# Row maxima of an attention kernel: split into high and low part on VectorE ahead of their turn, and one fp32r product with an identity in place of an fp32 transposition

## The chip, the core and the metric

The kernel runs on one core of a Trainium2 chip. TensorE multiplies matrices (128 rows by 128 columns of stationary weights, a moving operand of up to 512 columns) and writes to PSUM. VectorE (DVE), ScalarE (ACT) and GpSimd (POOL) do the elementwise work, and SyncE (SP) issues most of the DMAs. Each engine takes its instructions in program order, and semaphores order the engines against each other. The metric is the time of one execution on the device, in microseconds. Before the change it was 838.71 us, the median of three runs (838.14 to 839.35).

## What is computed

With `x` of 2048 x 640, everything in fp32:

```python
xn  = layernorm(x)
# A: 32 heads of 20, a causal window of 256 keys
q, k, v = heads(xn @ wqkv)
p   = softmax(where(0 <= i - j < 256, q @ k.T * 20**-0.5, -1e9))
s   = (p @ v).merge() @ wo
# B: squared ReLU
g   = silu(relu(xn @ w1 + b1)**2 @ w2 + b2)
out = x + s * g
```

## The kernel before

Products that need close to fp32 accuracy are made in fp32r, with each operand split into a rounded high part and a rest (`hi`, `lo`), and three of the four cross products are summed. `P` = 128, `BT` = 512, `HP` = 64.

The attention runs over 16 pairs of heads (`NP`) and 16 tiles of 128 queries (`NT`), 256 steps in all, plus 11 steps in which the last ones run out. A step `s` does four things in this order on TensorE:

- `scores` (L644): for both heads of the pair, the scores of query tile `q` against up to 384 keys, queries in rows. They serve only to find the row maximum.
- `scores_t` (L684), 9 steps later (`LAG`) for the same tile: the scores again, keys in rows. The stationary and moving operands have two rows more than the 60 of the three-part split (62): the two parts of minus the maximum, so that the product comes out as score minus maximum.
- at every fourth step, `max_rows` (L659): the maxima of the four query tiles just finished are turned from a column per tile into rows.
- then "filler": the products of the other linear layers (`halves`, L634), as many as a planner's clock allows, and on some steps a burst of `values` (L725).

The two heads of a pair, and two jobs of the filler, lie in different halves of TensorE's rows: rows 0 to 63 and rows 64 to 127. The two halves work at the same time on different products. Below they are called **the first half** and **the second half** of the array. `both(one, two, cost)` issues a product for each, and charges `cost` to the planner's clock of each half. The order of all instructions is laid down by Python code at build time (`manual_schedule`): `fill(due[s] + ...)` issues filler until the planner's clock has reached the step's due time. `COST` is the planner's assumption of what a product takes, by its moving columns; it is not measured while the kernel runs.

The path of the maxima before the change:

- `maxima` (L652, DVE): adds the mask to the scores, takes the maximum along the row, and reads the accumulator into one column of `mts`, a 128 x 64 tile of which 8 columns are used (4 query tiles, 2 heads). Two such tiles alternate. Each reduction is two DVE instructions, `CUSTOM_DVE_ANT_0` and `DVE_READ_ACCUMULATOR2_ANT`. The reduction also frees the PSUM bank that the next step's `scores` writes into, so that `scores` of step `s` waits for `maxima` of step `s-1`.
- `max_rows` (L659, PE): two fp32 transpositions of 64 x 64, one per half of the rows, into a corner of the PSUM tile `stps` that `scores_t` of the same step uses.
- ACT L665 takes the 8 rows out of PSUM with the sign turned, ACT L666 rounds them to fp32r (high part), POOL L667 subtracts to get the low part, and two DMAs (L669) put both into rows 60 and 61 of each head's half of `qs`, where `scores_t` finds them three steps later.

The PSUM tile `stps` has one buffer, so `scores_t` of the next step waits until ACT has read it (L690, the exponential, and L665).

Of the kernel before, what the change touches and what calls it, by code (L numbers as in the profile page):

```python
# [9 lines left out]
F32 = mybir.dt.float32  # L10
F32R = mybir.dt.float32r
BF16 = mybir.dt.bfloat16
AF = mybir.ActivationFunctionType
ALU = mybir.AluOpType

P = 128
# [9 lines left out]
BT = S // NB  # L26
VW = DH + 1
NPART = 3
KR = NPART * DH
HP = P // 2  # L30
HALF = D // 2
# [7 lines left out]
EARLY_FILL = 0.4  # L39
WARM = 22  # L40
WARM2 = 10
COST = {P: 0.067, 2 * P: 0.12, HALF: 0.147, 3 * P: 0.172, BT: 0.23}
SCALE = DH ** -0.5
PV = 0.2133
TURN = 0.18
# [12 lines left out]
def f32(ap):  # L58
    return ap.bitcast(F32)
# [3 lines left out]
def attn_mlp_kernel(ctx: ExitStack, tc, x, wqkv, wo, w1, b1, w2, b2, out):  # L63
    nc = tc.nc
    PSUM = bass.MemoryType.PSUM
    const = ctx.enter_context(tc.tile_pool(name="const", bufs=1))
# [27 lines left out]
    ident = const.tile([P, P], F32, name="ident")  # L94
    nc.gpsimd.memset(ident, 1.0)
    nc.gpsimd.affine_select(ident, ident, pattern=[[1, P]], compare_op=ALU.is_equal, fill=0.0, base=0, channel_multiplier=-1)
    mask = const.tile([P, 3 * P], F32, name="mask")
# [1 line left out]

    nc.gpsimd.affine_select(mask[:, 0:P], mask[:, 0:P], pattern=[[1, P]], compare_op=ALU.is_gt, fill=NEG, base=0, channel_multiplier=-1)  # L100
    nc.gpsimd.affine_select(mask[:, 2 * P:], mask[:, 2 * P:], pattern=[[-1, P]], compare_op=ALU.is_ge, fill=NEG, base=0, channel_multiplier=1)
    mts = [const.tile([P, HP], F32, name=f"mt{j}") for j in range(2)]
    for t_ in mts:
        nc.gpsimd.memset(t_, 0.0)
    ones = const.tile([2, P], F32, name="ones")
    nc.gpsimd.memset(ones, 1.0)
    eps = const.tile([P, 1], F32, name="eps")
# [12 lines left out]
    qs = [at.tile([P, S], F32R, tag="qs0", name="qs0")]  # L120
# [457 lines left out]
    at2 = ctx.enter_context(tc.tile_pool(name="at2", bufs=2))  # L578
# [16 lines left out]
    def put(j, emit, cost):  # L595
        clock[2] = clock[j]
        clock[j] += cost
        emit()
# [11 lines left out]
    def ahead(emit, cost):  # L610
        while clock[1] <= clock[0] + LEAD:
            if not open_for(backlog):
                clock[1] = max(clock[1], clock[0])
                break
            behind(backlog)
        put(0, emit, cost)
# [7 lines left out]
    def both(first, second, cost):  # L624
        ahead(first, cost)
        put(1, second, cost)
# [9 lines left out]
    def scores(p, q):  # L636
# [5 lines left out]
        def one(hh):  # L642
            o = slice(hh * HP, hh * HP + KR)
            nc.tensor.matmul(ss[hh][:, :nk], qs[i][o, q * P:(q + 1) * P], ks[i][o, k0 * P:k0 * P + nk], start=True, stop=True)  # L644
        both(lambda: one(0), lambda: one(1), COST[nk])
        return ss, nk

    def maxima(p, q, ss, nk):
        for hh in range(2):
            junk = at2.tile([P, 3 * P], BF16, tag="junk", bufs=1, name="junk")  # L650
            m = 4 * hh + q % 4
            nc.vector.tensor_tensor_reduce(out=junk[:, :nk], in0=ss[hh][:, :nk], in1=mask[:, 3 * P - nk:], scale=1.0, scalar=-3.0e38, op0=ALU.add, op1=ALU.max, accum_out=mts[q // 4 % 2][:, m:m + 1])  # L652

    def max_rows(p, g, tps):
        i = p % 2

        def one(j):
            r = slice(j * HP, (j + 1) * HP)
            nc.tensor.transpose(tps[:HP, j, 3 * P:3 * P + HP], mts[g % 2][r, :], ident[r, r])  # L659
        both(lambda: one(0), lambda: one(1), COST[P])  # L660

        def rest():
            row = at2.tile([8, P], F32, tag="row", bufs=1, name="row")
            mrow = at2.tile([8, 2, P], F32R, tag="mrow", bufs=1, name="mrow")
            nc.scalar.activation(row.rearrange("m (j n) -> m j n", j=2), tps[:8, :, 3 * P:3 * P + HP], AF.Copy, scale=-1.0)  # L665
            nc.scalar.activation(mrow[:, 0, :], row, AF.Copy)  # L666
            nc.gpsimd.tensor_sub(mrow[:, 1, :], row, f32(mrow[:, 0, :]))  # L667
            for a in range(2):
                nc.sync.dma_start(f32(qs[i])[KR + a:KR + a + HP + 1:HP, g * BT:(g + 1) * BT].rearrange("h (q n) -> h q n", q=4), f32(mrow)[:, a, :])  # L669
        return rest  # L670

    pts = {}
# [1 line left out]
    def pair_tile():  # L674
        return ptp.tile([P, 2, BT], F32, tag="st", name="stps")

    def scores_t(p, kb):
# [4 lines left out]
        def one(hh):  # L682
            o = slice(hh * HP, hh * HP + KR + 2)
            nc.tensor.matmul(tps[:, hh, :n], ks[i][o, kb * P:(kb + 1) * P], qs[i][o, kb * P:kb * P + n], start=True, stop=True)  # L684
        both(lambda: one(0), lambda: one(1), COST[n])
        return tps, n
# [11 lines left out]
    def bursts(p):  # L698
        return (range(0, 8), range(8, NT)) if p < NP - 1 else [range(4 * g, 4 * g + 4) for g in range(NB)]

    def burst_at(p, kb):
        return next((ts for ts in bursts(p) if ts[-1] == kb), None)
# [10 lines left out]
    def burst_cost(ts):  # L713
        return TURN + PV * max(sum(len(part) for e, _, part in lanes_of(ts) if e == e_) for e_ in range(2))
# [104 lines left out]
    def halves(job, ps, a, b_, first, last, o=0, n=None):  # L819
        n = n or ps.n  # L820
        cost, out = COST[n], ps.tile[:, o:o + n]

# [564 lines left out]
    def stretch(s):  # L1387
        ts = burst_at(*divmod(s - LAG - PLAG, NT)) if s >= LAG + PLAG else None
        return max(0.0, burst_cost(ts) - 1.8) if ts else 0.0

    total = (8 * (KC - 1) * 15 * COST[BT] + 2 * NB * (15 * (WIDE * COST[BT] + 2 * (NFH - WIDE) * COST[MT]) + 8 * 18 * COST[HALF]) + NP * 2 * NT * COST[3 * P] + sum(burst_cost(r) for p in range(NP) for r in bursts(p)))
    pace = (total - sum(stretch(s) for s in range(steps))) / (steps - 1)
# [16 lines left out]
    with tc.manual_schedule(engines={E_.PE, E_.Activation, E_.DVE, E_.Pool, E_.SP}):  # L1409
# [4 lines left out]
        def at_step(n):  # L1414
            return divmod(n, NT) if 0 <= n < NP * NT else None

        for s in range(steps):
# [7 lines left out]
            a, b, e = (at_step(s - lag) for lag in (0, LAG, LAG + PLAG))  # L1425
            if a:
                p, q = a
# [12 lines left out]
            rows = None  # L1440
# [4 lines left out]
            if s % 4 == 0 and 0 < s <= NP * NT:  # L1445
                rows = max_rows((s - 1) // NT, (s - 1) % NT // 4, stp[0] if b else pair_tile())
            if a:
                maxima(*a, *sc)
# [9 lines left out]
            r = e and burst_at(*e)  # L1458
# [41 lines left out]
```

## Time and profile before

| | |
|---|---|
| median of three runs | 838.71 us |
| the profiled execution | 838.47 us, of which the span from the first to the last instruction is 836.7 us |
| granted TensorE clock, mean | 0.999 |
| TensorE matmul busy, share of the span | 827.1 us, 99% |
| VectorE busy | 479.9 us, 57% |
| ScalarE busy | 438.5 us, 52% |
| GpSimd busy | 379.4 us, 45% |
| DMA traffic | 166.44 MB, 199 GB/s |

A matmul's record begins when it is issued to the array and ends by a model, so its duration (0.3 to 0.4 us for the common shapes) is longer than the time after which the next one starts on the same rows. What a product costs is read from the distance between starts on one half. "PEld" is TensorE's weight load. In a row of the timeline, the columns are start, duration (both us), engine, line, operation, the tile written and those read, the shape, and the number of merged instructions.

### The profile page before, as it was taken

To read this page: it belongs to the slowest core of one execution; us is meant where nothing else is said; L and a number is where in the kernel's file an instruction comes from. 1 tells how busy PE (TensorE), PEld (TensorE's weight loads), DVE (VectorE), ACT (ScalarE), POOL (GpSimd) and SP (SyncE) were. 2 spreads that over 40 slices of the span, in tenths; PEclk is the share of its full clock that TensorE was granted. 3 is DMA by queue.
4 is the path that set the end of the run, shared out by engine and by line. 5 is a ranking of instruction groups with operands and counts; after the bars stand their busy time and mean duration, and the time that the engine had idled before them with its cause. 6 is when DMAs were issued, how large, how long until landed. Compare 5 with 4: busy or idle time off the path is not lost.

```text
span 836.7 us, 25540 instructions
## 1 busy us (share of the span) xinstructions
PE 827.1 (99%) x10152; PEld 778.4 (93%) x10152; DVE 479.9 (57%) x1398; ACT 438.5 (52%) x824; POOL 379.4 (45%) x704
## 2 busy tenths in 40 slices
PE   8999999999999999999999999999999999999997
PEld 8999999988888999999999999899999999999997
DVE  7755457656577645455455476754455454446764
ACT  6253325545566754763754765844654744764321
POOL 5167902434334643553543553643543643552543
PEclk9999999999999999999999999999999999999999
DMA  6999578879889456355356254486375375356962
GB/s 236 307 389 341 178 203 277 272 234 288 278 287 307 124 161 174 85 183 144 87 194 183 72 164 143 129 249 175 88 227 172 86 221 171 94 160 207 383 203 80
DMA packets 88944, 166.44 MB, mean 199 GB/s; under 512 B 10360, under 2 KB 36600, under 8 KB 87800
## 3 DMA queue, kind: packets, MB, share of 16 engines
q1 hardware_dynamic: 88664, 164.63, 62.6%
q8 instruction: 80, 1.31, 0.7%
q14 instruction: 40, 0.33, 0.1%
q10 hardware_dynamic: 160, 0.16, 0.1%
HBM read 93.66 MB, written 70.52 MB: 196 GB/s over the span
## 4 chain that ended last, share of the span: by engine, by line
PE 96%; DVE 2%; issue 1%; DMA 0%; ACT 0%; DVEq 0%
PE yps L634 21%; PE hps L634 19%; PE qkps L634 14%; PE ops L725 10%; PE wops L794 8%; PE stps L684 5%; PE sps L644 5%; PE vps L235 4%; PE qkps L210 3%; PE vps L356 3%; PE tps L177 1%; DVE junk L652 1%; DVE w L985 1%; PE vps L411 0%; PE vps L401 0%
## 5 line engine op out<-in xcount | busy, mean ns | idle before, releaser
L652 DVE CUSTOM_DVE_ANT_0 junk<-sps,mask 128x384 bf16<-128x384 f32 (+2 forms) x512 | 272.1, 531 | 255.4 <-PE sps L644 92.4
L690 ACT ACTIVATE p<-stps 128x768 f32<-128x768 f32 (+2 forms) x256 | 197.5, 772 | 249.4 <-PE stps L684 204.7
L691 POOL TENSOR_SCALAR_AFFINE_SELECT p<-p 128x256 f32<-128x256 f32 x256 | 110.4, 431 | 317.5 <-ACT p L690 312.8
L634 PE MATMUL yps<-w,hh 64*128 64x320 f32 x1536 | 224.9, 309 | 1.8 <-ACT relu L1144 0.9
L634 PE MATMUL hps<-xb,w 64*128 64x256 f32 (+1 forms) x2100 | 210.7, 304 | 0.0
L634 PEld LDWEIGHTS hps<-xb,w 64*128 64x128 f32 x2100 | 194.5, 186 | 3.1 <-issue 2.5
L634 PEld LDWEIGHTS yps<-w,hh 64*128 64x128 f32 x1536 | 185.7, 185 | 5.0 <-DVE ysb L1179 1.7
L634 PE MATMUL yps<-w,hl 64*128 64x320 f32 x768 | 175.2, 309 | 0.0
L644 PE MATMUL sps<-ks,qs 60*128 60x384 f32 (+2 forms) x512 | 130.9, 335 | 0.8 <-DVE mt L652 0.6
L684 PE MATMUL stps<-qs,ks 62*128 62x384 f32 (+2 forms) x512 | 127.6, 334 | 0.1
L634 PEld LDWEIGHTS yps<-w,hl 64*128 64x128 f32 x768 | 117.4, 185 | 1.1 <-issue 1.0
L634 PE MATMUL qkps<-xT,wgkh 64*128 64x512 f32 x320 | 100.3, 393 | 0.0
L634 PE MATMUL qkps<-xT,wgqh 64*128 64x512 f32 x320 | 98.5, 392 | 0.0
L693 POOL TENSOR_SCALAR_AFFINE_SELECT p<-p 128x256 f32<-128x256 f32 x224 | 95.9, 428 | 0.0
L725 PE MATMUL ops<-p,vp 128*21 128x128 f32 (+1 forms) x2128 | 86.6, 311 | 0.0
L644 PEld LDWEIGHTS sps<-ks,qs 60*128 60x128 f32 x512 | 81.1, 185 | 5.2 <-DVE mt L652 2.9
L725 PEld LDWEIGHTS ops<-p,vp 128*21 128x21 f32 x2128 | 63.5, 101 | 21.1 <-issue 6.2
L684 PEld LDWEIGHTS stps<-qs,ks 62*128 62x128 f32 x512 | 80.9, 187 | 1.0 <-issue 0.3
L1149 POOL TENSOR_TENSOR hl<-sq,hh 128x512 fp32r<-128x512 f32 x48 | 62.1, 1294 | 17.8 <-ACT sq L1148 17.6
L794 PE MATMUL wops<-wo,oT 128*128 128x320 f32 x384 | 61.9, 310 | 0.0
L634 PE MATMUL qkps<-xT,wgkl 64*128 64x512 f32 x160 | 61.6, 393 | 0.0
L634 PE MATMUL qkps<-xT,wgql 64*128 64x512 f32 x160 | 61.3, 392 | 0.0
(163 smaller groups left out, 1288.8 us busy)
## 6 DMA issues: line engine op xcount, KB each, us to landing
ks<-k_d SPq DMA_DIRECT2D x64, 240.0 KB
qs<-q_d SPq DMA_DIRECT2D x64, 240.0 KB
xb<-xs SPq DMA_DIRECT2D x60, 256.0 KB
k_d<-shm SPq DMA_DIRECT2D x20, 512.0 KB
q_d<-shm SPq DMA_DIRECT2D x20, 512.0 KB
xs<-xT SPq DMA_DIRECT2D x8, 1280.0 KB
y<-ysb SPq DMA_DIRECT2D x28, 320.0 KB
o<-osb SPq DMA_DIRECT2D x64, 128.0 KB
```

What stands on the lines that cost most here:

```text
L210: nc.tensor.matmul(ps, wt[:, c, :], xT[part][b][:, c * BT + t0:c * BT + t0 + n], start=m == 1, stop=m == 3 * KC)
L235: nc.tensor.matmul(ps, xT[xp][b][:, c * BT + t * P: c * BT + (t + 1) * P], wv[wp][:, c, nh * HALF:(nh + 1) * HALF], start=first and m == 0 ...
L634: return nc.tensor.matmul(out, a[r], b_[r], skip_group_check=True, **kw)
L644: nc.tensor.matmul(ss[hh][:, :nk], qs[i][o, q * P:(q + 1) * P], ks[i][o, k0 * P:k0 * P + nk], start=True, stop=True)
L652: nc.vector.tensor_tensor_reduce(out=junk[:, :nk], in0=ss[hh][:, :nk], in1=mask[:, 3 * P - nk:], scale=1.0, scalar=-3.0e38, op0=ALU.add, o ...
L684: nc.tensor.matmul(tps[:, hh, :n], ks[i][o, kb * P:(kb + 1) * P], qs[i][o, kb * P:kb * P + n], start=True, stop=True)
L690: nc.scalar.activation(p32[:, :, :n], tps[:, :, :n], AF.Exp, scale=SCALE)
L691: nc.gpsimd.affine_select(p32[:, :, 0:P], p32[:, :, 0:P], pattern=[[0, 2], [1, P]], compare_op=ALU.is_ge, fill=0.0, base=0, channel_multip ...
L693: nc.gpsimd.affine_select(p32[:, :, 2 * P:], p32[:, :, 2 * P:], pattern=[[0, 2], [-1, P]], compare_op=ALU.is_gt, fill=0.0, base=0, channel ...
L725: nc.tensor.matmul(ot[r0:r0 + VW, c0:c0 + len(part), :], vps[p][:, kb // 4, kb % 4, hh, :], pts[p, kb][:, hh, :].rearrange("p (t n) -> p t ...
L794: nc.tensor.matmul(ps, a, b_, start=j == 0, stop=j == n - 1)
L1149: nc.gpsimd.tensor_sub(hh[1][:, :BT], sq, f32(hh[0]))
```

## The change

- The maxima of one group (4 query tiles, 2 heads) go to a tile `tops` of 8 columns. At every fourth step, right after the last reduction, VectorE copies `tops` to columns 0 to 7 of `parts`, rounded to fp32r, and writes the rest into columns 8 to 15. `parts` is 128 x 128 with zeros elsewhere, set once from a part of the mask that is zero; there is one of it.
- `max_rows` is one fp32r product per half, with `parts` (64 rows x 128 columns) as the stationary operand and a 64 x 64 identity `eye` in fp32r as the moving one. It writes 128 PSUM rows instead of 64; the first 16 are used.
- One ACT instruction takes all 16 rows out. The second ACT instruction and the POOL subtraction are gone. The two DMAs stay.
- The planner charges 0.04 for the product, where it charged 0.067 for the transposition.

```diff
-COST = {P: 0.067, 2 * P: 0.12, HALF: 0.147, 3 * P: 0.172, BT: 0.23}
+COST = {HP: 0.04, P: 0.067, 2 * P: 0.12, HALF: 0.147, 3 * P: 0.172, BT: 0.23}
...
-    mts = [const.tile([P, HP], F32, name=f"mt{j}") for j in range(2)]
-    for t_ in mts:
-        nc.gpsimd.memset(t_, 0.0)
+    tops = const.tile([P, 8], F32, name="tops")
+    parts = const.tile([P, P], F32R, name="parts")
+    nc.scalar.activation(parts, mask[:, P:2 * P], AF.Copy)
+    eye = const.tile([P, HP], F32R, name="eye")
+    for h in (slice(0, HP), slice(HP, P)):
+        nc.scalar.activation(eye[h], ident[h, h], AF.Copy)
...
-            nc.vector.tensor_tensor_reduce(..., accum_out=mts[q // 4 % 2][:, m:m + 1])
+            nc.vector.tensor_tensor_reduce(..., accum_out=tops[:, m:m + 1])
+        if q % 4 == 3:
+            nc.vector.tensor_copy(parts[:, 0:8], tops)
+            nc.vector.tensor_sub(parts[:, 8:16], tops, f32(parts[:, 0:8]))
...
-            nc.tensor.transpose(tps[:HP, j, 3 * P:3 * P + HP], mts[g % 2][r, :], ident[r, r])
-        both(lambda: one(0), lambda: one(1), COST[P])
+            nc.tensor.matmul(tps[:, j, 3 * P:3 * P + HP], parts[r, :], eye[r, :], start=True, stop=True, skip_group_check=True)
+        both(lambda: one(0), lambda: one(1), COST[HP])
...
-            nc.scalar.activation(row.rearrange("m (j n) -> m j n", j=2), tps[:8, :, 3 * P:3 * P + HP], AF.Copy, scale=-1.0)
-            nc.scalar.activation(mrow[:, 0, :], row, AF.Copy)
-            nc.gpsimd.tensor_sub(mrow[:, 1, :], row, f32(mrow[:, 0, :]))
+            nc.scalar.activation(rows.rearrange("m (j n) -> m j n", j=2), tps[:16, :, 3 * P:3 * P + HP], AF.Copy, scale=-1.0)
```

How this moves the instructions is shown for one group, the one whose transposition starts at 430.82 us in the trace. On TensorE, before: the last filler products ahead of the step, the two score products, the two transposed ones, the two transpositions (`x2`), and filler again.

```order
L634 MATMUL yps<-w_0_1_4001,hh 128x320
L644 MATMUL sps<-ks_117,qs_116 128x384 [waits DVE_49] x2
L684 MATMUL stps<-qs_1478,ks_1479 128x384 [waits Activation_49]
L684 MATMUL stps<-qs_1478,ks_1479 128x384
L659 MATMUL stps<-ident,mt_100 64x64 x2
L634 MATMUL yps<-w_0_0_3964,hh 128x320
L634 MATMUL yps<-w_0_0_3964,hl 128x320
```

The same place on TensorE after the change:

```order
L637 MATMUL yps<-w_0_2_4181,hh 128x320
L647 MATMUL sps<-ks_119,qs_118 128x384 [waits DVE_49] x2
L687 MATMUL stps<-qs_1480,ks_1481 128x384 [waits Activation_49]
L687 MATMUL stps<-qs_1480,ks_1481 128x384
L665 MATMUL stps<-eye,parts 128x64 [waits DVE_49]
L665 MATMUL stps<-eye,parts 128x64
L637 MATMUL yps<-w_0_1_3991,hh 128x320
L637 MATMUL yps<-w_0_0_3950,hl 128x320
```

The product stands where the transpositions stood, and it has a wait for VectorE of its own; the transpositions had none. The filler around it is a little further on in its list than before.

On VectorE, before: the last two reductions of the group and the first two of the next, with their accumulator reads, at the same place.

```order
L652 ISA junk,mt_100<-sps,mask 128x384 [waits DVE_49,PE_49]
L652 ISA mt_100 128x1
L652 ISA junk,mt_100<-sps,mask 128x384 [waits DVE_49,PE_49]
L652 ISA mt_100 128x1
L652 ISA junk,mt_101<-sps,mask 128x384 [waits DVE_49,PE_49]
L652 ISA mt_101 128x1
L652 ISA junk,mt_101<-sps,mask 128x384 [waits DVE_49,PE_49]
L652 ISA mt_101 128x1
L1179 TENSOR_TENSOR ysb<-yps,b2t 128x320 [waits PE_49]
```

The same place on VectorE after the change:

```order
L655 ISA junk,tops<-sps,mask 128x384 [waits DVE_49,PE_49]
L655 ISA tops 128x1
L655 ISA junk,tops<-sps,mask 128x384 [waits DVE_49,PE_49]
L655 ISA tops 128x1
L657 CAST parts<-tops 128x8 [waits DVE_49]
L658 TENSOR_TENSOR parts<-tops,parts 128x8 [waits DVE_49]
L1182 TENSOR_TENSOR ysb<-yps,b2t 128x320 [waits PE_49]
L655 ISA junk,tops<-sps,mask 128x384 [waits DVE_49,PE_49]
L655 ISA tops 128x1
```

Two short instructions stand between the last reduction of a group and whatever VectorE does next, and each waits for the one before it on its own engine (`DVE_49`).

On ScalarE, before: the exponential of this step, the two instructions of the maxima, and the exponential of the next step.

```order
L690 ACTIVATE p_7546<-stps 128x768 [waits PE_49]
L665 ACTIVATE row<-stps 8x128 [waits Pool_49]
L666 ACTIVATE mrow<-row 8x128 [waits DMAHW7_49,DMAHW0_49,Activation_49]
L690 ACTIVATE p_7600<-stps 128x768 [waits PE_49]
L690 ACTIVATE p_7647<-stps 128x768 [waits PE_49]
```

The same place on ScalarE after the change:

```order
L693 ACTIVATE p_7533<-stps 128x768 [waits PE_49]
L670 ACTIVATE rows<-stps 16x128 [waits DMAHW7_49,DMAHW0_49]
L693 ACTIVATE p_7582<-stps 128x768 [waits PE_49]
L693 ACTIVATE p_7626<-stps 128x768 [waits PE_49]
L693 ACTIVATE p_7672<-stps 128x2x256 [waits PE_49]
```

One of the two is left, and it no longer waits for GpSimd.

More of the change, by code (lines that the diff above doesn't have):

```diff
@@ L651, in maxima @@
             m = 4 * hh + q % 4
-            nc.vector.tensor_tensor_reduce(out=junk[:, :nk], in0=ss[hh][:, :nk], in1=mask[:, 3 * P - nk:], scale=1.0, scalar=-3.0e38, op0=ALU.add, op1=ALU.max, accum_out=mts[q // 4 % 2][:, m:m + 1])
+            nc.vector.tensor_tensor_reduce(out=junk[:, :nk], in0=ss[hh][:, :nk], in1=mask[:, 3 * P - nk:], scale=1.0, scalar=-3.0e38, op0=ALU.add, op1=ALU.max, accum_out=tops[:, m:m + 1])
+        if q % 4 == 3:
+            nc.vector.tensor_copy(parts[:, 0:8], tops)
+            nc.vector.tensor_sub(parts[:, 8:16], tops, f32(parts[:, 0:8]))
     def max_rows(p, g, tps):
@@ L658, in one @@
             r = slice(j * HP, (j + 1) * HP)
-            nc.tensor.transpose(tps[:HP, j, 3 * P:3 * P + HP], mts[g % 2][r, :], ident[r, r])
-        both(lambda: one(0), lambda: one(1), COST[P])
+            nc.tensor.matmul(tps[:, j, 3 * P:3 * P + HP], parts[r, :], eye[r, :], start=True, stop=True, skip_group_check=True)
+        both(lambda: one(0), lambda: one(1), COST[HP])
         def rest():
-            row = at2.tile([8, P], F32, tag="row", bufs=1, name="row")
-            mrow = at2.tile([8, 2, P], F32R, tag="mrow", bufs=1, name="mrow")
-            nc.scalar.activation(row.rearrange("m (j n) -> m j n", j=2), tps[:8, :, 3 * P:3 * P + HP], AF.Copy, scale=-1.0)
-            nc.scalar.activation(mrow[:, 0, :], row, AF.Copy)
-            nc.gpsimd.tensor_sub(mrow[:, 1, :], row, f32(mrow[:, 0, :]))
+            rows = at2.tile([16, P], F32R, tag="rows", bufs=1, name="rows")
+            nc.scalar.activation(rows.rearrange("m (j n) -> m j n", j=2), tps[:16, :, 3 * P:3 * P + HP], AF.Copy, scale=-1.0)
             for a in range(2):
-                nc.sync.dma_start(f32(qs[i])[KR + a:KR + a + HP + 1:HP, g * BT:(g + 1) * BT].rearrange("h (q n) -> h q n", q=4), f32(mrow)[:, a, :])
+                nc.sync.dma_start(f32(qs[i])[KR + a:KR + a + HP + 1:HP, g * BT:(g + 1) * BT].rearrange("h (q n) -> h q n", q=4), f32(rows)[8 * a:8 * a + 8])
         return rest
```

## The prediction

> **What bounds the kernel now.** First the page: busy shares, then the chain that ended last.
>
> ```profile
> PE 827.1 (99%) x10152; PEld 778.4 (93%) x10152; DVE 479.9 (57%) x1398; ACT 438.5 (52%) x824; POOL 379.4 (45%) x704
> ...
> PE 96%; DVE 2%; issue 1%; DMA 0%; ACT 0%; DVEq 0%
> ```
>
> TensorE is busy throughout and holds 96% of the chain. So what the change takes off ScalarE, GpSimd and the DMA path of the maxima is worth nothing unless TensorE waits for it. What counts is the time that the two products of a group occupy on TensorE, and any time TensorE now has to wait. Next the view of waits, for what TensorE and its weight load wait for.
>
> ```profile
> PEld sps L644 <- DVE mt L652: 2.9, 9, 0.5
> ...
> PEld yps L634 <- ACT relu L1144: 1.4, 2, 0.8
> ```
>
> The waits shown are small (total, count, longest, in us), and the larger one is for VectorE's maxima. But the view counts only time in which no modelled record runs, and records last 0.3 us and more, so waits below that hide in it. They have to be read from starts. Here is one group, first VectorE and then TensorE.
>
> ```profile
> 429.69 0.08 DVE L652 DVE_READ_ACCUMULATOR2_ANT mt<- 128x1 f32 x1
> 429.92 0.56 DVE L652 CUSTOM_DVE_ANT_0 junk<-sps,mask 128x384 bf16<-128x384 f32 x1
> 430.40 0.08 DVE L652 DVE_READ_ACCUMULATOR2_ANT mt<- 128x1 f32 x1
> 430.88 0.56 DVE L652 CUSTOM_DVE_ANT_0 junk<-sps,mask 128x384 bf16<-128x384 f32 x1 [0.40 <-PE yps L634]
> ```
>
> ```profile
> 430.54 0.43 PE L684 MATMUL stps<-qs,ks 62*128 62x384 f32 x1
> 430.65 0.34 PE L644 MATMUL sps<-ks,qs 60*128 60x384 f32 x1
> 430.82 0.22 PE L659 MATMUL stps<-ident,mt 64*64 64x64 f32 x1
> 430.83 0.33 PE L684 MATMUL stps<-qs,ks 62*128 62x384 f32 x1
> 430.85 0.39 PE L634 MATMUL yps<-w,hh 64*128 64x320 f32 x1
> 431.00 0.22 PE L659 MATMUL stps<-ident,mt 64*64 64x64 f32 x1
> 431.03 0.39 PE L634 MATMUL yps<-w,hl 64*128 64x320 f32 x1
> 431.08 0.31 PE L634 MATMUL yps<-w,hh 64*128 64x320 f32 x1
> 431.23 0.30 PE L634 MATMUL yps<-w,hl 64*128 64x320 f32 x1
> ```
>
> The last reduction of the group ends at 429.92 + 0.56 = 430.48, and the transposition in the first half of the array starts only 0.34 us later. It needs nothing more from VectorE: `scores` of that step has already waited for the same reduction. The interval is the time of the products ahead of it.
>
> **The price of the product itself.** After the transposition (430.82) the next product of that half is issued 0.03 us later, but is 0.08 longer than others of its shape (0.39 against 0.31), and the second next starts at 431.08. Two plain products follow each other by 431.23 - 431.08 = 0.15. So the transposition occupies its half for 431.08 - 430.82 - 0.15 = 0.11. An fp32r product of 64 columns isn't in the trace; the nearest has 128.
>
> ```profile
> 188.26 0.22 PE L644 MATMUL sps<-ks,qs 60*128 60x128 f32 x1
> ...
> 188.32 0.39 PE L684 MATMUL stps<-qs,ks 62*128 62x384 f32 x1
> ...
> 188.55 0.22 PE L659 MATMUL stps<-ident,mt 64*64 64x64 f32 x1
> ```
>
> The pattern is the same: the next product is issued 0.06 later, is too long by about 0.05, and the one after it starts 0.23 later, where a 384-column product is normally followed after 0.18 (430.65 to 430.83). A 128-column product thus occupies 0.06 + 0.05 = 0.11 as well. Equal cost at 64 columns of fp32 and 128 of fp32r says that the columns don't set it; I read it as the next product's weight load, which begins when this one starts. The bounds: at the lowest, the 0.08 belongs to the transposition alone and the new product costs 0.03, which saves 64 groups x 0.08 = 5.1 us; at the highest it costs the 0.11 of the 128-column row. I take 0.11, **a gain of 0**.
>
> The stationary operand grows from 64 to 128 columns. Its load is hidden behind a 384-column product ahead of it, but in 15 groups (step 16p + 24, where `scores_t` is at its last tile) that product has 128 columns.
>
> ```profile
> 246.02 0.22 PE L684 MATMUL stps<-qs,ks 62*128 62x128 f32 x1
> ...
> 246.08 0.22 PE L659 MATMUL stps<-ident,mt 64*64 64x64 f32 x1
> 246.11 0.47 PE L634 MATMUL qkps<-xT,wgqh 64*128 64x512 f32 x1
> ```
>
> Today the transposition starts 0.06 after it, so its narrow load fits. With 128 columns the excess of the row above (0.05 to 0.06) comes in: 15 x 0.057 = **0.9 us lost**; at least 0, at most 15 x 0.11 = 1.7.
>
> [...]
>
> **The wait that is added.** The product needs `parts`, which VectorE finishes with a copy and a subtraction after the group's last reduction. Prices of short VectorE instructions come from one operation at two sizes, and the pause before a dependent one from the start of the kernel:
>
> ```profile
> L114 DVE TENSOR_TENSOR xT<-tps,xT 128x512 fp32r<-128x512 f32 x15 | 9.2, 680 | 1.1 <-ACT xT L113 1.1
> ...
> L471 DVE TENSOR_TENSOR xT<-tps,xT 128x128 fp32r<-128x128 f32 x4 | 1.1, 280 | 0.0
> ```
>
> ```profile
> 6.01 0.11 DVE L455 RECIPROCAL rstd<-rstd 128x1 f32<-128x1 f32 x1
> 6.15 0.61 DVE L162 TENSOR_SCALAR xn<-xt,mv,rstd 128x640 f32<-128x640 f32 x1
> ```
>
> (680 - 280) / 384 = 1.04 ns per column, so 8 columns take 280 - 120 x 1.04 = 155 ns; the reciprocal of one column, 110, is the lower neighbour. A dependent instruction starts 0.03 after an ordinary one (6.15 - 6.12), but 0.15 after an accumulator read (429.77 to 429.92). From the end of the reduction: 0.15 + 0.155 + 0.035 + 0.155 = 0.50. From there to TensorE I take what `scores` needs in the next rows, 0.06 (449.78 to 449.84), and then the load of 128 columns, 0.11. The product can start to work about **0.66 us after the last reduction**. Short end: 0.03 + 0.08 (a read) + 0.03 + 0.155 + 0.06 + 0.11 = 0.47. Long end: 0.85, with 0.2 for each instruction and 0.15 for both pauses.
>
> Where does the transposition stand today? Three groups:
>
> ```profile
> 449.22 0.56 DVE L652 CUSTOM_DVE_ANT_0 junk<-sps,mask 128x384 bf16<-128x384 f32 x1
> ...
> 449.84 0.44 PE L644 MATMUL sps<-ks,qs 60*128 60x384 f32 x1
> ...
> 450.12 0.22 PE L659 MATMUL stps<-ident,mt 64*64 64x64 f32 x1
> ```
>
> ```profile
> 625.23 0.56 DVE L652 CUSTOM_DVE_ANT_0 junk<-sps,mask 128x384 bf16<-128x384 f32 x1
> ...
> 626.18 0.22 PE L659 MATMUL stps<-ident,mt 64*64 64x64 f32 x1
> ```
>
> ```profile
> 496.71 0.56 DVE L652 CUSTOM_DVE_ANT_0 junk<-sps,mask 128x384 bf16<-128x384 f32 x1
> ...
> 498.57 0.22 PE L659 MATMUL stps<-ident,mt 64*64 64x64 f32 x2
> ```
>
> The distance is 450.12 - 449.78 = 0.34 in the first, 0.39 in the second, 1.30 in the third. Over all 64 groups the first half's distance runs from 0.34 to 1.30: 26 groups lie below 0.46, none between 0.46 and 0.58, and 33 below 0.66. In those, TensorE reaches the product before `parts` is there, and it takes its instructions in order: behind the waiting product stand its twin in the second half and all filler, so both halves run dry. Taking 0.66 less the distance wherever positive gives 8.1 us in the first half. The second half's transposition comes later (450.29, not 450.12), so with 0.68 it loses in 23 groups only, 3.0 us. Which counts? The halves' starts stay in program order, and the earlier half loses mostly a lead that it would have given up at the next point where both meet; so I go near the later one and take **3.5 us**. With the short end, 0.47, the sums are 2.8 and 0.03; with the long end, 15.8 and 8.5.
>
> **The rest.** VectorE gets 64 x 0.35 = 22 us more, at 57% busy. Its next reductions and PSUM evacuations come up to 0.35 later at those 64 places; TensorE's own wait covers this in the groups above, and elsewhere VectorE idles there (0.40 us before the reduction at 430.88). If that cover were gone, a late free bank would cost up to 0.3 each time. ScalarE loses one instruction per group and GpSimd one:
>
> ```profile
> L666 ACT ACTIVATE mrow<-row x64: 308/310/312, 123.4 to 734.5; 8x128 fp32r<-8x128 f32 x64
> L667 POOL TENSOR_TENSOR mrow<-row,mrow x64: 442/451/458, 123.9 to 735.1; 8x128 fp32r<-8x128 f32 x64
> ```
>
> That is 20 and 29 us of work off engines that TensorE seldom waits for, and rows that arrive 0.7 us sooner, three steps ahead of their use: 0, at most the 2 us or so that the view of waits shows for ScalarE. The two DMAs stay and no longer hold SP for GpSimd: 0. The planner's 0.067 - 0.04, 64 times, lets 1.7 us of filler go out earlier; the work is the same, the places shift: 0, plus or minus 1.
>
> **Sum.** Against the profiled execution (836.7 span, 838.47 in all): 0 + 0.9 + 3.5 = +4.4, 842.9. The median of the runs is 0.24 higher, so **843.1 us**.
>
> **Rivals.**
> (A) Not slower: the wait is there but hidden, since the chain is near its short end and lost time is made up within the half. Against it speaks the 0.15 after an accumulator read; for it, that only the first half is exposed at 0.47. It gives 838.7 + 0.03 + 0.9 = 839.6, no change.
> (B) The other side: the 0.08 is the transposition's own, and an fp32r product costs 0.03. Its place is the first product after each transposition, its price 64 x 0.08 = 5.1 us, and it decides as soon as more is saved than waits cost (4.4). With the waits as forecast it gives 838.0, with the short end 834.5. The 128-column row speaks against it. [...]
> (C) The chain is near its long end: 8.5 + 0.9 gives 848.1. A longer start of the copy would do it.
>
> **How the numbers follow.** Forecast 0.55, A 0.27, B 0.10, C 0.08. A measurement of this kernel can tell 0.2%, 1.7 us. The forecast and C are slower (0.63); A is within (0.26, with a little of B); B's lower part and a rest are faster (0.11). The range takes in the forecast, A, the upper part of B and C up to its centre: 837.0 to 848.0; about 0.15 lies outside.
>
> **What would show it.** In the profile of the changed kernel: the product's start after the last reduction never under about 0.5 us (now 0.34), with many groups bunched there; products following it still about 0.08 too long; copy and subtraction near 0.15 each with 0.15 ahead of the copy; TensorE's span in the attention longer by some us, ACT and POOL busy 20 and 29 us less. It is wrong if the bunch lies at 0.35, if the next product after it starts without delay, or if VectorE's reductions move so late that whole steps shift.

## The result, and the profile after

The changed kernel takes **857.05 us**, the median of five runs (856.88 to 858.63), against 838.71 us before. The ratio, taken over all runs of both, is 1.0225, with a 95% interval of 1.0214 to 1.0236: 18 to 20 us slower, where +4.4 was forecast. The profiled execution took 857.06 us, with a span of 855.3 us at a mean granted clock of 1.0 (0.999 before), so the clock has no part in it. Of the experiments below, two of the eleven executions of the product alone without the selects ran at a granted clock of 0.56 and 0.57 and took 1341.28 and 1313.63 us, and they are left out of its comparison. First the page of the changed kernel: busy times, and the chain that ended last, by engine and by line.

```profile
PE 841.1 (98%) x10152; PEld 785.1 (92%) x10152; DVE 514.2 (60%) x1526; ACT 423.6 (50%) x764; POOL 346.4 (40%) x638
...
PE 90%; DVE 8%; issue 1%; DMA 0%; ACT 0%; DVEq 0%
PE yps L637 18%; PE hps L637 18%; PE qkps L637 13%; PE ops L728 10%; PE wops L797 8%; PE sps L647 4%; PE vps L238 4%; DVE junk L655 4%; PE stps L687 4%; PE qkps L213 3%; PE vps L359 3%; DVE parts L657 1%; PE stps L665 1%; DVE parts L658 1%; PE tps L180 1%
```

The share that says most is VectorE's in the chain: 8%, from 2%. The copy (L657) and the subtraction (L658) stand in it by name, and so do the reductions ahead of them (L655). VectorE is busy 514.2 - 479.9 = 34 us longer, for 128 short instructions that were forecast at 64 x 0.35 = 22 us. ScalarE is busy 438.5 - 423.6 = 15 us less and GpSimd 33 us less, and the time is longer all the same.

Next the waits of TensorE and its weight load in the changed kernel (total us, count, longest).

```profile
PEld stps L665 <- DVE parts L658: 12.9, 31, 1.1
PEld yps L637 <- DVE ysb L1182: 3.9, 8, 0.8
...
PE stps L665 <- DVE parts L658: 1.7, 6, 0.9
```

The wait for `parts` is there, 31 times and up to 1.1 us. A second line has also grown: filler that waits for a PSUM evacuation (`ysb`), 3.9 us where it was 1.7. What the two added instructions take is in the view of the tile `parts` (duration in ns: shortest, median, longest).

```profile
L665 PEld LDWEIGHTS stps<-eye,parts x128: 182/183/188, 122.5 to 753.1; 64*128 64x128 f32 x128
L665 PE MATMUL stps<-eye,parts x128: 189/293/295, 122.6 to 753.1; 64*128 64x64 f32 x128
L657 DVE CAST parts<-tops x64: 170/367/851, 121.9 to 752.3; 128x8 fp32r<-128x8 f32 x64
L658 DVE TENSOR_TENSOR parts<-tops,parts x64: 166/316/1179, 122.1 to 752.7; 128x8 fp32r<-128x8 f32 x64
```

The shortest are near the 155 ns of the prediction; the medians are twice that. An operation of fixed shape whose time runs from 170 to 851 is being held by something. Here is one group of the changed kernel in the timeline, the one whose step stood at 430.82 us before.

```profile
439.08 0.56 DVE L655 CUSTOM_DVE_ANT_0 junk<-sps,mask 128x384 bf16<-128x384 f32 x1
...
439.56 0.08 DVE L655 DVE_READ_ACCUMULATOR2_ANT tops<- 128x1 f32 x1
439.63 0.41 POOL L694 TENSOR_SCALAR_AFFINE_SELECT p<-p 128x256 f32<-128x256 f32 x1 [3.16 <-ACT p L693]
439.68 0.39 DVE L657 CAST parts<-tops 128x8 fp32r<-128x8 f32 x1
...
439.99 0.41 POOL L696 TENSOR_SCALAR_AFFINE_SELECT p<-p 128x256 f32<-128x256 f32 x1
440.00 0.33 PE L687 MATMUL stps<-qs,ks 62*128 62x384 f32 x1
440.10 0.32 DVE L658 TENSOR_TENSOR parts<-tops,parts 128x8 fp32r<-128x8 f32 x1
...
440.34 0.48 DVE L1182 TENSOR_TENSOR ysb<-yps,b2t 128x320 f32<-128x320 f32 x1
440.47 0.18 PEld L665 LDWEIGHTS stps<-eye,parts 64*128 64x128 f32 x2 [0.46 <-DVE parts L658]
440.47 0.30 PE L665 MATMUL stps<-eye,parts 64*128 64x64 f32 x2
440.58 0.19 PEld L637 LDWEIGHTS yps<-w,hh 64*128 64x128 f32 x1
```

Read it downwards. The reduction ends at 439.64 and the copy starts at 439.68, almost at once. But GpSimd has been in its first select (L694, it masks the exponentials) since 439.63. That ends at 440.04, and the copy ends at 440.07. The subtraction starts 0.03 later, under the second select (L696), which ends at 440.40; the subtraction ends at 440.42. Each ends 0.02 to 0.03 after a select does. So it is with all that are long: 50 of the 64 copies and 48 of the 64 subtractions took over 200 ns, all 98 started while a GpSimd instruction was running, and all ended 16 to 29 ns after it (96 times a select, twice a longer subtraction of GpSimd's, `hl`, L1152). TensorE's weight load, idle for 0.46, starts at 440.47: 0.83 after the last reduction, which is also the median over the 64 groups. With 0.11 for the load, counted to the start of the next one (440.47 to 440.58; the load's own record lasts 0.18), the product works from 0.94 on, by estimate; 0.66 was forecast.

The lengths of the steps, worked out from the first start of `scores` in each and summed by the step's place in a group of four (without the very first step), show where the time is. The step of the product is number 0; the bursts of `values` make step 2 the longest.

| us | step 0 | step 1 | step 2 | step 3 |
|---|---|---|---|---|
| before | 149.9 | 145.8 | 188.0 | 131.5 |
| after | 167.4 | 147.6 | 186.5 | 133.7 |

Nearly all of it, 17.5 us, is in the steps of the product. What remained was to split that: the product itself, the wait for `parts`, VectorE's own delay, and what GpSimd does to both.

### The profile page after: what moved, and what is told of

Read it like the earlier page. It is cut to its first block, busy times and chain, and to the rows that moved or that the text cites. A ratio compares the mean times of both kernels' runs of the same rounds, so it can differ in the third digit from the quotient of the medians.

```text
span 855.3 us, 25611 instructions
## 1 busy us (share of the span) xinstructions
PE 841.1 (98%) x10152; PEld 785.1 (92%) x10152; DVE 514.2 (60%) x1526; ACT 423.6 (50%) x764; POOL 346.4 (40%) x638
## 4 chain that ended last, share of the span: by engine, by line
PE 90%; DVE 8%; issue 1%; DMA 0%; ACT 0%; DVEq 0%
PE yps L637 18%; PE hps L637 18%; PE qkps L637 13%; PE ops L728 10%; PE wops L797 8%; PE sps L647 4%; PE vps L238 4%; DVE junk L655 4%; PE stps L687 4%; PE qkps L213 3%; PE vps L359 3%; DVE parts L657 1%; PE stps L665 1%; DVE parts L658 1%; PE tps L180 1%
## 5 line engine op out<-in xcount | busy, mean ns | idle before, releaser
L655 DVE CUSTOM_DVE_ANT_0 junk<-sps,mask 128x384 bf16<-128x384 f32 (+2 forms) x512 | 272.0, 531 | 237.6 <-PE sps L647 106.2
L694 POOL TENSOR_SCALAR_AFFINE_SELECT p<-p 128x256 f32<-128x256 f32 x256 | 107.0, 418 | 403.5 <-ACT p L693 398.0
L637 PE MATMUL hps<-xb,w 64*128 64x256 f32 (+1 forms) x2100 | 208.3, 304 | 1.0 <-DVE ysb L1182 1.0
L637 PEld LDWEIGHTS hps<-xb,w 64*128 64x128 f32 x2100 | 190.3, 186 | 6.1 <-issue 2.7
L637 PE MATMUL yps<-w,hl 64*128 64x320 f32 x768 | 180.2, 309 | 0.0
L637 PEld LDWEIGHTS yps<-w,hl 64*128 64x128 f32 x768 | 122.4, 185 | 0.8 <-issue 0.8
L647 PE MATMUL sps<-ks,qs 60*128 60x384 f32 (+2 forms) x512 | 117.4, 335 | 0.0
L687 PE MATMUL stps<-qs,ks 62*128 62x384 f32 (+2 forms) x512 | 114.6, 333 | 0.0
L637 PE MATMUL qkps<-xT,wgqh 64*128 64x512 f32 x320 | 100.6, 394 | 0.0
L696 POOL TENSOR_SCALAR_AFFINE_SELECT p<-p 128x256 f32<-128x256 f32 x224 | 93.1, 416 | 0.0
L647 PEld LDWEIGHTS sps<-ks,qs 60*128 60x128 f32 x512 | 72.1, 185 | 2.7 <-DVE tops L655 1.0
L687 PEld LDWEIGHTS stps<-qs,ks 62*128 62x128 f32 x512 | 70.8, 187 | 0.8 <-ACT p L693 0.2
L1152 POOL TENSOR_TENSOR hl<-sq,hh 128x512 fp32r<-128x512 f32 x48 | 62.8, 1308 | 16.7 <-ACT sq L1151 16.7
```

Source lines behind the costliest of these rows:

```text
L637: return nc.tensor.matmul(out, a[r], b_[r], skip_group_check=True, **kw)
L694: nc.gpsimd.affine_select(p32[:, :, 0:P], p32[:, :, 0:P], pattern=[[0, 2], [1, P]], compare_op=ALU.is_ge, fill=0.0, base=0, channel_multip ...
L696: nc.gpsimd.affine_select(p32[:, :, 2 * P:], p32[:, :, 2 * P:], pattern=[[0, 2], [-1, P]], compare_op=ALU.is_gt, fill=0.0, base=0, channel ...
L1152: nc.gpsimd.tensor_sub(hh[1][:, :BT], sq, f32(hh[0]))
```

## The experiments

All are medians of 4 to 11 executions, compared with runs of the kernel before on the same chip (838.06, 838.12 or 837.98 us).

### The product, and the planner's price

**Only the price.** The kernel before, with the price of the new product for the transposition.

```diff
-COST = {P: 0.067, 2 * P: 0.12, HALF: 0.147, 3 * P: 0.172, BT: 0.23}
+COST = {HP: 0.04, P: 0.067, 2 * P: 0.12, HALF: 0.147, 3 * P: 0.172, BT: 0.23}
...
-        both(lambda: one(0), lambda: one(1), COST[P])
+        both(lambda: one(0), lambda: one(1), COST[HP])
```

> The kernel before, with the planner's price of the transposition lowered from 0.067 to 0.04 and nothing else: only the places of the filler shift. If the 18 us come from TensorE standing at the product until VectorE has finished the split (theory W), this stays at 838.7 within 1.5 us. If the new order of the filler costs the time (rival: order), it is at least 5 us slower.

839.68 against 838.06: 1.0020 (1.0012 to 1.0029), 1.0 to 2.4 us. The moved filler costs something, and is a small part of the loss.

**The product alone.** The changed kernel without copy and subtraction; the product reads a `parts` that stays zero, so that no maximum is subtracted from the scores, and waits for nothing.

```diff
-        if q % 4 == 3:
-            nc.vector.tensor_copy(parts[:, 0:8], tops)
-            nc.vector.tensor_sub(parts[:, 8:16], tops, f32(parts[:, 0:8]))
```

> The changed kernel without the copy and the subtraction: the products read a constant tile of zeros, so no maximum is subtracted from the scores, and the products wait for nothing. W: 837.5 to 840.5, the 838.7 of before with at most 0.9 for the wider weight load. Rival: the product itself is dearer than the transposition (each by 0.28 us, 64 times): about 857, whether it waits or not.

838.21: 1.0002 (0.9993 to 1.0010). This is also the ceiling of the idea in this schedule: with the split at no cost at all there is nothing to gain. The planner's new price, which cost 1.6 us in the run before, is in this kernel too, so something gives them back. It is not the product. Both kernels have the same filler around it, and in one group the transposition and the second filler product behind it on its half lie as far apart in the run before (first view) as the fp32r product and the same filler product do here (second view):

```profile
316.02 0.22 PE L659 MATMUL stps<-ident,mt 64*64 64x64 f32 x1
316.29 0.30 PE L634 MATMUL yps<-w,hh 64*128 64x320 f32 x1
```

```profile
315.10 0.20 PE L662 MATMUL stps<-eye,parts 64*128 64x64 f32 x1
315.36 0.30 PE L637 MATMUL yps<-w,hh 64*128 64x320 f32 x1
```

That is 0.27 and 0.26: the product costs what the transposition cost. What is left between the two runs is the work taken off ScalarE and GpSimd and the earlier rows; which of them gives the 1.5 us back is open. The extra load behind short products, forecast at 0.9, is not there: in the 15 groups with 128 columns ahead the product starts 0.060 us after them in the median, the transposition 0.062. The waits of TensorE in this run are the yardstick for the next ones:

```profile
PEld yps L637 <- DVE ysb L1179: 1.9, 4, 0.5
...
PEld sps L647 <- DVE tops L655: 1.0, 4, 0.3
...
PE yps L637 <- DVE ysb L1179: 0.8, 3, 0.3
```

### VectorE's time, and GpSimd

**The split made, but not read.** Copy and subtraction go to a tile that nobody reads; the product reads zeros as above.

```diff
...
-            nc.vector.tensor_copy(parts[:, 0:8], tops)
-            nc.vector.tensor_sub(parts[:, 8:16], tops, f32(parts[:, 0:8]))
+            nc.vector.tensor_copy(spare[:, 0:8], tops)
+            nc.vector.tensor_sub(spare[:, 8:16], tops, f32(spare[:, 0:8]))
```

> The changed kernel with the copy and the subtraction into a tile that nobody reads; the products read a constant tile of zeros (no maximum is subtracted) and wait for nothing. W: as without the two instructions, 838 to 841.5. Rival: VectorE's own delay, that is reductions and evacuations that come up to 0.8 us later 64 times: 848 or more.

846.68: 1.0100 (1.0084 to 1.0115). Nobody waits for the split, and 8.5 us are lost all the same (846.68 - 838.21), between what was expected and its rival, nearer the rival. TensorE's waits in this run:

```profile
PEld yps L638 <- DVE ysb L1183: 4.8, 9, 0.7
PEld sps L648 <- DVE tops L656: 2.7, 10, 0.5
PE yps L638 <- DVE ysb L1183: 2.5, 8, 0.5
PEld hps L638 <- DVE ysb L1183: 1.9, 3, 0.9
```

Filler waits for evacuations (4.8 for 1.9, and for `hps` 1.9 for 0.2) and `scores` for reductions (2.7 for 1.0, though it was 2.9 in the kernel before, so this line alone says little). The reductions of step 0 end 0.32 us later behind their `scores` than with no split. The cost of VectorE's delay, set at 0 in the prediction, is almost half of the loss. The rows add up to less than 8.5, since the view hides waits under a matmul's record; how it divides between the two stays open. By the steps it is 3.6 us in step 0 of the group, 2.0 in step 1, 0.1 in the long step 2 and 2.9 in step 3.

**Without the selects of that step.** The changed kernel, and GpSimd leaves out both selects of the exponentials in the last step of each group, the one in which the split runs.

```diff
         nc.scalar.activation(p32[:, :, :n], tps[:, :, :n], AF.Exp, scale=SCALE)
+        if kb % 4 == 2:
+            pts[p, kb] = p32
+            return
```

> The changed kernel without GpSimd's two masking instructions in the last step of each group (every fourth key tile stays unmasked). If the copy and the subtraction last 0.37 and 0.32 because GpSimd works on SBUF at the same time, they fall to 0.17 each in nearly all groups, the weight load of the product can begin 0.47 us after the last reduction instead of 0.83, and by the sums over the groups of before 4 to 6 us remain in the first half and 0.2 to 1 in the second: 840 to 846. If the two instructions are long for a reason of their own, they stay at 0.37 and 0.32, and the time at 857.

846.51: 1.0099 (1.0085 to 1.0113), so 10.5 of the 18 to 19 us are gone; the expected range ended at 846. In the tile's view the medians fall to the minima, while the product is the same:

```profile
L657 DVE CAST parts<-tops x64: 170/172/1257, 123.4 to 743.1; 128x8 fp32r<-128x8 f32 x64
L658 DVE TENSOR_TENSOR parts<-tops,parts x64: 166/168/171, 123.6 to 743.3; 128x8 fp32r<-128x8 f32 x64
```

And the same group as above, in the timeline of this run:

```profile
435.50 0.56 DVE L655 CUSTOM_DVE_ANT_0 junk<-sps,mask 128x384 bf16<-128x384 f32 x1
...
436.10 0.17 DVE L657 CAST parts<-tops 128x8 fp32r<-128x8 f32 x1
...
436.31 0.17 DVE L658 TENSOR_TENSOR parts<-tops,parts 128x8 fp32r<-128x8 f32 x1
...
436.53 0.19 PEld L665 LDWEIGHTS stps<-eye,parts 64*128 64x128 f32 x2
```

From the reduction's end (436.06) to the load it is 0.47, not 0.83, and TensorE's load no longer waits in this group. Two copies are still long, 1257 and 851 ns, without any select in that step. The longer of them:

```profile
544.80 1.27 POOL L1155 TENSOR_TENSOR hl<-sq,hh 128x512 fp32r<-128x512 f32 x1 [0.56 <-ACT sq L1154]
...
544.84 1.26 DVE L657 CAST parts<-tops 128x8 fp32r<-128x8 f32 x1
```

It started under another GpSimd instruction, and both copies end 26 ns after that one does. So it is not the selects as such; another instruction of GpSimd's within SBUF does the same.

**Both together, and the control.** The unread split without the selects, and the product alone without the selects.

> The unread split of e3 (the products read a constant tile) without GpSimd's masking in the last step of each group: copy and subtraction at 0.17 each instead of 0.38 and 0.32, so 0.35 us less on VectorE per group and no wait at the product. If e3's 8.6 us follow the time that VectorE is held, about half goes: 841 to 844. If the number of instructions counts, it stays at 846 or 847. The difference from e4 (846.5, same but read) is the wait at the product with a short chain: 2 to 6 us.

> Control for e4 and e8: no split at all, products read a constant tile (no maximum is subtracted), and GpSimd's masking in the last step of each group left out. 837 to 839, so that the missing masking by itself is worth less than 1 us against e2 (838.2).

842.29: 1.0047 (1.0035 to 1.0059), and 837.74: 0.9998 (0.9989 to 1.0008). Without the split the selects are worth nothing to the time; they matter through VectorE. The five runs make a table:

| us | split not made | made, not read | made and read |
|---|---|---|---|
| with the selects | 838.2 | 846.7 | 857.05 |
| without them | 837.7 | 842.3 | 846.5 |

Each difference is good to about 1.5 us. Along the upper row: VectorE's delay costs 8.5, and reading the split, with the wait at the product, 10.4 more. Along the lower: 4.6 and 4.2. So 10 of the 19 us come from the two instructions being held while GpSimd's selects run, and they come from both terms.

How much is delay and how much is wait in the changed kernel itself can only be bounded, from starts. From `scores` of the product's step to the product, summed over 63 groups, it is 21.0 us for the earlier of the two products and 20.5 for the later, with no split and with the unread one alike; in the changed kernel it is 35.8 and 28.7. The wait is therefore 8.2 to 14.8 us, by the half that one goes by. Of the 18.7 us that all steps are longer than with no split, 4 to 10 are left for VectorE's delay. The 10.4 and 8.5 of the table lie within these bounds.

### The place

**Same work, another place.** As many unread copies and subtractions, two pairs after the reductions of every eighth query tile, ahead of a burst of `values`. They read zeros of the mask.

```diff
...
-        if q % 4 == 3:
-            nc.vector.tensor_copy(parts[:, 0:8], tops)
-            nc.vector.tensor_sub(parts[:, 8:16], tops, f32(parts[:, 0:8]))
+        for _ in range(2 if q % 8 == 2 else 0):
+            nc.vector.tensor_copy(spare[:, 0:8], mask[:, P:P + 8])
+            nc.vector.tensor_sub(spare[:, 8:16], mask[:, P:P + 8], f32(spare[:, 0:8]))
```

> The same number of unread copies and subtractions as in e3 (their source is a constant zero tile), but two pairs at a time in the steps that carry a burst of values products, where VectorE idles for some 2.5 us; products read a constant tile. If e3's 8.6 us come from what stands behind the split on VectorE in a short step (reductions, evacuations), they vanish: 837.5 to 840. If VectorE's added work costs wherever it stands (or disturbs GpSimd): 843 to 847.

838.47: 1.0004 (0.9995 to 1.0013). Half of the instructions are as short here as without the selects:

```profile
L658 DVE CAST spare<-mask x64: 165/172/1216, 119.7 to 721.8; 128x8 fp32r<-128x8 f32 x64
L659 DVE TENSOR_TENSOR spare<-mask,spare x64: 166/169/318, 119.9 to 722.2; 128x8 fp32r<-128x8 f32 x64
```

The medians hide the other half: 31 copies and 30 subtractions took over 200 ns here, so that the 128 instructions take 31.8 us in all, against 23.6 in the unread split without the selects and 39.5 in the one with them. Those cost 4.6 and 8.5 us; here, with a time between the two, it is 0.3. VectorE's 43% of idle time is cover enough in the long steps with a burst, and not in the short ones.

**Product a step later.** The changed kernel with the product at the next step, when `parts` is ready; and as a control the kernel before with its transposition moved in the same way.

```diff
-            if s % 4 == 0 and 0 < s <= NP * NT:
-                rows = max_rows((s - 1) // NT, (s - 1) % NT // 4, ...)
+            if s % 4 == 1 and 1 < s <= NP * NT + 1:
+                rows = max_rows((s - 2) // NT, (s - 2) % NT // 4, ...)
```

> The changed kernel with the product one step later (steps 4k+1 instead of 4k), so that the split has a whole step of some 2.4 us more. The unread split cost 8.6 us without any wait, and the whole change 18.9, so two parts are assumed: VectorE's delay and TensorE's wait at the product. If they add, the wait goes and VectorE's part stays: 845 to 848. If the wait was the whole and the unread split cost its 8.6 us by chance of order: 838 to 841.

> The kernel before with its transposition one step later, as a control of that shift: 836.5 to 840, since the transposition waited for nothing.

848.88: 1.0126 (1.0111 to 1.0141), and the control 852.82: 1.0180 (1.0159 to 1.0202), which is a miss. The control's waits say why, for most of it: the rows of the maxima reach `qs` too late.

```profile
PE stps L684 <- DMA qs<-mrow: 8.9, 7, 2.7
```

The later place has a price of its own in the control. In the first of the two runs, whose rows take a shorter way, the same wait is only 0.3 us, and no wait for `parts` is left. It is 8.2 us better than the changed kernel and 2.2 above the unread split (its expected range ended at 848). That fits a wait removed and VectorE's delay left; with no control that has the same rows it does not prove it.

**The split off VectorE.** The later product again, with the copy on ScalarE and the subtraction on GpSimd, both after the exponentials, and two `tops` tiles that alternate.

```diff
...
+    def split_tops(q):
+        t_ = tops[q // 4 % 2]
+        nc.scalar.activation(parts[:, 0:8], t_, AF.Copy)
+        nc.gpsimd.tensor_sub(parts[:, 8:16], t_, f32(parts[:, 0:8]))
...
```

> The product one step later as in e5, and the split on other engines: the rounding on ScalarE after the exponential of the group's last step, the subtraction on GpSimd behind its masking, two tiles of maxima in turn. VectorE has nothing added. If VectorE's delay is what stays in e5, this is at 837 to 840; if the product or the shift costs it, it stays at e5's time.

844.88: 1.0089 (1.0066 to 1.0111), with six executions from 842.5 to 849.3. By the medians it is 4 us better than with VectorE, but above what was expected; late rows and late exponentials both show among the waits:

```profile
PE stps L689 <- DMA qs<-rows: 1.2, 2, 1.0
PEld stps L689 <- ACT p L695: 1.2, 2, 0.9
```

**Product in the middle of its step.** Same step, but after the first part of the filler, so that `parts` is ready and the rows are not a whole step late; once with the split on VectorE, once on ScalarE and GpSimd.

```diff
...
+            if s % 4 == 0 and 0 < s <= NP * NT:
+                fill(due[s] + 0.7 * pace)
+                max_rows((s - 1) // NT, (s - 1) % NT // 4, ...)()
```

> The changed kernel with the product behind some 1.3 us of filler in the same step, so that the split is ready when TensorE gets there, and the rows are late by 1 us only (e6 lost 14.7 by rows that came too late). The wait at the product goes, VectorE's part stays: 846 to 849. If the two parts don't add, it is nearer 840 or stays at 857.

> As e11, with the split on ScalarE and GpSimd behind the last exponential and masking of the group, and two tiles of maxima in turn: neither the wait nor VectorE's added work. 838 to 842; it can't beat e2 (838.2), which has no split at all, by more than noise.

855.12: 1.0203 (1.0189 to 1.0217), and 858.11: 1.0246 (1.0232 to 1.0260). Both miss widely. In the first of them the waits for `parts` are gone and others have come:

```profile
PEld stps L665 <- ACT p L693: 4.2, 11, 1.4
...
PEld stps L687 <- ACT rows L670: 2.8, 7, 0.8
```

The product writes into `stps`, which the exponential of the step is reading by then, and the next `scores_t` waits until ScalarE has taken the rows out. With the split off VectorE the first of these is TensorE's own:

```profile
PE stps L667 <- ACT p L695: 5.3, 11, 1.4
```

At its first place the product shares the tile with `scores_t`, ahead of the exponential, and has no such wait. The waits shown, 7 us in the first run, are less than half of what is lost against 838; VectorE's delay may be in the rest, which no run here divides. A PSUM tile of its own for the product was not tried. No version here beats the kernel before.

## Why the prediction was right or wrong

**The sign: right,** and one half of the mechanism, a product that reaches TensorE before `parts`. The size was 857.06 - 838.47 = 18.6 us against 4.4, outside the range. Two steps failed: the chain to the product was mis-sized (0.94 us in place of 0.66), and the delay of what stands behind it on VectorE was put at 0. The terms one by one:

- **The product at the transposition's price: right.** The product alone gives 838.21, and the starts around it are the same. With it rival B falls, a product at 0.03: its 5.1 us less are outside the interval.
- **The load behind short products, 0.9: not there.** The product starts 0.060 us after the short one, as the transposition did (0.062).
- **"8 columns take 280 - 120 x 1.04 = 155 ns": mis-sized.** The alone-running instruction is close (170 and 166), and the long end allowed 0.2. But the row came from a subtraction that takes one of its sources from PSUM, and what GpSimd does meanwhile was not asked. The two new instructions read only SBUF, and the schedule puts them under the selects: 367 and 316 ns. The trace of before had a hint, in an SBUF-only subtraction of the same engine:

```profile
L1310 DVE TENSOR_TENSOR ob<-ob,sums 128x768 f32<-128x768 f32 x8 | 11.7, 1466 | 0.0
L1310 DVE TENSOR_TENSOR ob<-ob,sums 128x512 f32<-128x512 f32 x8 | 5.5, 682 | 0.0
```

By the prediction's own slope, 512 columns take 280 + 384 x 1.04 = 679 and 768 take 946. The second row agrees, the first is 1.5 times as long, and its mean mixes two cases. In the two places where GpSimd is idle the 768 columns take 951 ns. In the other six they take 1637 ns, start while an addition of GpSimd's is running (`res`, L1380), and end 0.82 us after it; 768 x 1.04 is 0.80. That fits an instruction whose data begin to move only when GpSimd is done. It works the other way as well:

```profile
L1380 POOL TENSOR_TENSOR res<-res,xres x30: 877/885/1267, 764.7 to 828.4; 128x320 f32<-128x320 f32 x30
```

The additions that start under such a VectorE subtraction (L1310 and L1314) are those of 1253 to 1267 ns, and no others. So the trace of before showed the hold, in both directions. The question to ask of a new instruction was not only how long it takes but beside what it runs.

- **"The pause before a dependent one", 0.15 after an accumulator read: wrong, and small.** The copy starts 0.035 after the read in all 64 groups. The 0.14 to 0.15 belongs to the next reduction. This error made the forecast too slow. The parts of the long end, "0.85", add up to 0.87 (0.15 + 0.2 + 0.15 + 0.2 + 0.06 + 0.11).
- **"I go near the later one and take 3.5 us": the 3.5 was too small because of the 0.66; the choice of the half is not decided.** With 0.94 and 0.96 in place of 0.66 and 0.68, the prediction's sums over the distances of before are 20.6 us for the first half and 12.2 for the second, and 10.4 was measured, near the later one. Without the selects, at 0.47 + 0.11 = 0.58 and 0.60, they are 5.6 and 1.3, and 4.2 was measured, nearer the first. With the right length of the chain alone the forecast would have been some 12 us.
- **"TensorE's own wait covers this ... and elsewhere VectorE idles there", cost 0: the step that failed in kind.** Where TensorE does not wait at the product, it is 8.5 us with the held instructions and 4.6 with short ones; in the changed kernel, where some of it lies under the wait, 4 to 10. The idle 0.40 us that was quoted as cover is one place after one group; a share of 57% busy is an average over long steps that have cover and short ones that have too little. The prediction named the price, "a late free bank would cost up to 0.3 each time": 64 times 0.3 would be 19 us, and up to half of that came.
- **Relief of ScalarE and GpSimd, 0, and the planner's drift, 0 plus or minus 1:** the first is consistent with the product alone, where at most the 1.5 us of the planner's price came back, the second was 1.6 by itself, a little outside.

Rival C, a chain near its long end at 848.1, was the nearest, but for another reason than the one given, "a longer start of the copy". What all cases lacked was two instructions that are long because of a third engine, and the second bill for the same delay.

## What to carry to other kernels

Before an operation is put on an engine with idle time, look at what the other engines do in that very stretch, and at an instruction of the same kind of operands there: the price of a short VectorE instruction doubled here under GpSimd's work (the copy took 170 ns alone and 367 in the median, the subtraction 166 and 316). Then bill the delay twice, at the consumer of the new result and at all that stands behind it on its own engine, taking the idle time of the step in question and not of the span. And test the ceiling first: with the split at no cost, this change could win nothing.

## What the runs showed of the hardware

- An 8-column copy of fp32 to fp32r within SBUF took 170 ns alone, up to 401 ns under GpSimd's selects of 0.41 us and 851 under a GpSimd subtraction of 1.3 us; the subtraction within SBUF 166, up to 319 and 1179. All 98 long ones in the changed kernel end 16 to 29 ns after the GpSimd instruction under which they started: that is waiting for it, not sharing with it. In the run without the selects the medians are 172 and 168 ns, in the changed kernel 367 and 316. The reductions, which read PSUM and the mask, are not stretched: 531 ns in the mean before and after, and 556 for those of 384 columns in the kernel before, whether GpSimd worked beside them or not. By what path the two engines hold each other no run here shows.
- The hold works in both directions: GpSimd's `res` addition took 877 to 885 ns alone and 1253 to 1267 where it started under a VectorE subtraction within SBUF.
- An fp32r product of 64 moving columns took the time of a 64 x 64 fp32 transposition: in one group 0.26 us from its start to the second product behind it on its half, and 0.27 with the transposition. Its load is of 128 columns, with records of 187 ns in the median, where the transposition's is of 64 columns and 108 ns; even so it started 0.060 us after a product of 128 columns, in the median of 15 groups, and the transposition 0.062.
